# Layer 2's first product as seven half-size products, with prepared factors streamed from DRAM

## The chip, the core and the metric

The kernel runs on one core of a Trainium2 chip. The metric is the device time of one execution in microseconds, as the median of several runs. The core has a matrix engine (TensorE, in the profile PE for matmuls and PEld for weight loads), a vector engine (DVE), a scalar engine (ACT), GpSimd (POOL) and a queue engine (SP), and 16 DMA engines that move data between DRAM and the on-chip memory SBUF. Matmuls write to PSUM, which has eight banks of 512 fp32 numbers per partition. Only DVE and ACT read PSUM here.

## The reference

```python
def _moe_ref(x, w_in, w_out):                 # layer 1
    h = x @ w_in                              # 3072 x 512 @ 512 x 2048
    g = h - np.tanh(h)
    return (g @ w_out).astype(np.float32)     # 3072 x 2048 @ 2048 x 512

def _moe2_ref(x, w_in, w_out, alpha):         # layer 2
    h = x @ w_in
    g = np.maximum(h, 0.0) + alpha * np.minimum(h, 0.0)
    return (g @ w_out).astype(np.float32)

def reference(**kwargs):
    ...
    attn_out = _attn_ref(**attn_kwargs)       # attention in chunks of 32 tokens, 4 x 8 heads x 768 x 64
    x = np.ascontiguousarray(attn_out.transpose(0, 2, 1, 3)).reshape(B * S, H * D)
    x = _moe_ref(x=x, **moe_kwargs)
    return _moe2_ref(x=x, **moe2_kwargs)
```

The weights arrive as 64-bit floats, which the kernel turns into fp32 by integer operations.

## The kernel before

The 3072 tokens are 24 tiles of 128. Both layers work through six blocks of four tiles (512 tokens), and within a block through 16 values of f, each of which stands for 128 of the 2048 hidden units. Layer 1 runs block by block first, then layer 2.

Every fp32 product is made of three matmuls: each operand is split into a high part and a low part (type fp32r), and the passes high x high, high x low and low x high are added up in PSUM (`PASS`). For one block and one f, `emit_h` issues 12 matmuls (four parts of the 512 inputs, three passes), each with 128 weight columns and 512 moving columns, into one bank of `ps_h`. `emit_g` applies the activation: in layer 2 DVE computes prelu in two operations (lines 191 and 194), ACT copies the high part gh (line 197), POOL subtracts it for the low part gl (line 198). `emit_y` issues 12 more matmuls, of 512 columns, into the four banks of `ps_y`, which collect y over the 16 values of f; in layer 2 these are on line 217. In the written order h of the next f comes ahead of y of this one. After the last f of a block `evac_y` copies the four banks out through tiles of the pool t (4 buffers): in layer 1 to y1d in DRAM by ACT's DMA queue, in layer 2 to the output by SP's.

The instructions of each engine are not issued strictly as written: the framework makes a schedule by its own estimates of durations, and an instruction that it holds ready can go ahead of one that it holds late. Each engine then runs its own list in order.

During layer 1 the attention of later tiles runs between the matmuls by a plan of due times (`both`, `emit_soft`, `tok_c`). In the blocks 1 to 4 of layer 1 every second step converts and splits one of the 32 weight tiles of layer 2 (`park`: ACT and three DVE operations in `to_f32`, then ACT and POOL in `split_f32`) and writes it to w2d in DRAM. In block 5 all of them are read back into SBUF (`unpark`), where they stay: 32 tiles of the pool w, which has 34 buffers of 4 KB per partition. For layer 2 `load_x2` reads a block of y1d and `split_x2` splits it into the ring of x operands with four ACT and four DVE operations.

Of the kernel before, what the change touches and what calls it, by code (L numbers as in the profile page):

```python
# [7 lines left out]
FP32 = mybir.dt.float32  # L8
FP32R = mybir.dt.float32r
# [10 lines left out]
PERIOD = 20  # L20
LP, SLACK, LAST_C = 3, 2, 5
SPACE = 6
SCB = 2
FIRST = 1
EARLY_W = (3, 4, 5)
ANCHOR = 'exp'
# [4 lines left out]
XF = 4  # L31
# [5 lines left out]
def chunk_attention_two_ffn_kernel(  # L37
# [27 lines left out]
    def f32(ap):  # L65
        return ap.bitcast(FP32)
# [11 lines left out]
    y1d = dr_p.tile([NTILE, 128, KD, 128], FP32, name="y1d")  # L78
    w2d = [dr_p.tile([128, 2 * 512], FP32, name=f"w2d{i}") for i in range(2 * NF)]

    wts = {}
    raws = {}
# [9 lines left out]
    def to_f32(raw):  # L92
# [12 lines left out]
        s = t_p.tile([128, 512], U32, tag="t", name="s")  # L105
# [9 lines left out]
    def keep(l, f, got):  # L115
        wts[l, f] = (got[0].rearrange("p a (k f) -> p a k f", k=KD), got[1])
# [7 lines left out]
            got.append(w)  # L124
        keep(l, f, got)

    def park(i):
        raw = raws.pop((1, i))
        w = raw.bitcast(FP32R)
        split_f32(to_f32(raw), w[:, 0:512], w[:, 512:1024])  # L130
        nc.sync.dma_start(out=w2d[i], in_=f32(w))

    def unpark(f):
        got = []
        for side in range(2):
            w = w_p.tile([128, 2, 512], FP32R, tag="w", name="wt")
            nc.sync.dma_start(out=f32(w).rearrange("p a n -> p (a n)"), in_=w2d[2 * f + side])
            got.append(w)
        keep(1, f, got)

    ring = [x_p.tile([128, RING, KD, 128], FP32R, name=f"ring{i}") for i in range(2)]

# [80 lines left out]
    def evac_y(l, b, n, t0):  # L223
        ys = yp.pop((l, b))
        for j, y in enumerate(ys):
            if l == 0:
                s = t_p.tile([128, 512], FP32, tag="t", name="ys")[:, :n * 128]
                src, dst = y[:, :n * 128], y1d[t0:t0 + n, :, j, :].rearrange("i p c -> p i c")
                so = s.rearrange("p (i c) -> p i c", i=n)
            else:  # L230
                s = t_p.tile([128, 512], FP32, tag="t", name="ys")
                src, dst, so = y, out[(t0 + j) * 128:(t0 + j + 1) * 128, :], s
            if j % 2 == 0:
                nc.scalar.activation(out=s, in_=src, func=ACTF.Copy)
            else:
                nc.vector.tensor_copy(out=s, in_=src)
            (nc.scalar if l == 0 else nc.sync).dma_start(out=dst, in_=so)

    x2 = {}

    def load_x2(b, n, t0):
        r = stage["x"].tile([128, max(blocks2), KD, 128], FP32, tag="x2", name="x2")
        nc.sync.dma_start(out=r[:, :n], in_=y1d[t0:t0 + n].rearrange("i p k c -> p i k c"))
        x2[b] = r

    def split_x2(b, n):
        r = x2.pop(b)
        for i in range(n):
            o = lambda c: ring[c][:, x0[1][b] + i]
            nc.scalar.activation(out=o(0), in_=r[:, i], func=ACTF.Copy)  # L250
            nc.vector.tensor_tensor(out=o(1), in0=r[:, i], in1=f32(o(0)), op=ALU.subtract)


    astack = ExitStack()
# [41 lines left out]
    def emit_scores(t):  # L296
        s = t % TPS
        kn = kt.pop(t)
        sp = ps_a.tile([128, 512], FP32, tag="a", name="sp")
        for p in range(HP):  # L300
            for c in range(4):
                last["at"] = nc.tensor.matmul(  # L302
                    out=sp[CH * c:CH * c + CH, 128 * p:128 * p + 128],
                    lhsT=qt[t][:, p, CH * c:CH * c + CH],
                    rhs=kn[p // 2][:, :, p % 2, c // 2, CH * (c % 2):CH * (c % 2) + W + NM],
                    start=True, stop=True,
                ).ins
# [5 lines left out]
        sc = aw.tile([128, H, 64], FP32, tag="sc", name="sc", bufs=SCB)  # L313
# [12 lines left out]
    def emit_soft(t):  # L326
        sc = sm.pop(t)
        sg = aw.tile([128, H, 1], FP32, tag="sg", name="sg")
        nc.vector.tensor_reduce(out=sg, in_=sc, op=ALU.add, axis=AX.X)
        nc.vector.tensor_scalar(out=sg, in0=sg, scalar1=1e-9, scalar2=None, op0=ALU.add)  # L330
        nc.vector.reciprocal(out=sg, in_=sg)
        nc.gpsimd.tensor_tensor(
            out=sc, in0=sc, in1=sg.to_broadcast([128, H, 64]), op=ALU.mult
        )
        et = aw.tile([128, H, 2, CH], FP32, tag="et", name="et", bufs=1)
# [70 lines left out]
        last["run"] = last["at"]  # L406

    slots = [(0, b, n, f) for b, n in enumerate(blocks1) for f in range(NF)]
    slots += [(1, b, n, f) for b, n in enumerate(blocks2) for f in range(NF)]
    N1 = len(blocks1)  # L410

    if True:
# [81 lines left out]
        for i, (l, b, n, f) in enumerate(slots):  # L494
            def attn(pos):
                if l == 0:
                    for fn, t in plan.pop(base[b] + pos, []):
                        fn(t)
                    return last.pop("run", None)

            if l == 0 and b == 0:
                more_w()
            if l == 0 and 0 < b < N1 - 1:
                n_park, at_step = divmod((b - 1) * NF + f, 2)
                if at_step == 0:
# [24 lines left out]

# [59 lines left out]
```

## Time and profile before

| | |
|---|---|
| Median of three runs | 1152.1 us (1151.5 to 1152.64) |
| The profiled execution | 1150.37 us |
| Its span, first to last instruction | 1148.5 us |
| PE busy | 1114.7 us (97%) in 6144 matmuls |
| PEld busy | 915.6 us (80%) |
| DVE, ACT, POOL busy | 485.5, 345.5, 363.1 us (42%, 30%, 32%) |
| Moved by DMA | 112.16 MB, 98 GB/s on average |

The profile is of one execution. Its span is a little shorter than the time that counts, since start and end of the program lie around it. Busy time is the union of an engine's records. Matmuls are pipelined, and a matmul's record holds its latency too, so the distance between the starts of matmuls in a row, their pitch, tells what one costs. Idle time on an engine that isn't the bottleneck costs nothing.

### The profile page before, as it was taken

The numbers are of one execution on the slowest core, as the hardware profiler recorded it, in microseconds if no ns is written. First come the engines' busy times: TensorE is split into PE (matmuls) and PEld (weight loads), VectorE is DVE, ScalarE is ACT, GpSimd is POOL, SyncE is SP. The second block draws the span as 40 slices with busy tenths as digits, with TensorE's granted clock in tenths as the row PEclk, the third lists the DMA queues.
The fourth block names the chain that finished last, engine by engine and source line by source line (L and its number), as shares of the span: only waits on it lengthen the run. The fifth ranks groups of instructions, "written<-read, shape, count | busy, mean of one in ns | idle before, by whom it ended". The sixth has DMA issues, their size and how long they took to land.

```text
span 1148.5 us, 15553 instructions
## 1 busy us (share of the span) xinstructions
PE 1114.7 (97%) x6144; PEld 915.6 (80%) x6144; DVE 485.5 (42%) x806; ACT 345.5 (30%) x612; POOL 363.1 (32%) x299
## 2 busy tenths in 40 slices
PE   3798999999999999999999999999999999999998
PEld 3587788888888887887888888888888888888886
DVE  6998635554554544553113224234224224322322
ACT  4665534444343444443222112112112112111111
POOL 4465533433243333332221222222222222222221
PEclk9699999999999999999999999999999999999999
DMA  9772334344444444436665002002002000000000
GB/s 256 260 271 81 104 115 142 125 150 138 147 144 151 140 135 145 149 109 222 204 198 183 1 1 74 1 1 74 1 1 67 7 1 19 19 1 13 25 1 37
DMA packets 53689, 112.16 MB, mean 98 GB/s; under 512 B 7281, under 2 KB 25713, under 8 KB 53617
## 3 DMA queue, kind: packets, MB, share of 16 engines
q1 hardware_dynamic: 40944, 104.89, 28.0%
q10 hardware_dynamic: 12672, 6.29, 1.9%
q8 instruction: 48, 0.79, 0.3%
q14 instruction: 25, 0.20, 0.1%
HBM read 81.80 MB, written 29.36 MB: 97 GB/s over the span
## 4 chain that ended last, share of the span: by engine, by line
PE 88%; DMA 4%; DVE 3%; issue 2%; SPq 1%; POOL 1%; ACT 0%; DVEq 0%; POOLq 0%; ACTq 0%
PE h L173 42%; PE y L217 23%; PE y L212 20%; PE pv L354 2%; PE sp L302 1%; DMA ri<-in_moe_w_in_dram 1%; DMA alpha_sb<-in_moe_alpha_dram 1%; DVE u L102 1%; DMA y1d<-ys 1%; SPq L276 1%; DVE s L106 1%; DVE u L99 1%; DVE ebuf L345 0%; DMA vn<-in_v_dram 0%; DMA w2d<-pk 0%
## 5 line engine op out<-in xcount | busy, mean ns | idle before, releaser
L173 PE MATMUL h<-ring,wt 128*128 128x512 f32 x2304 | 561.2, 392 | 8.9 <-DVE t L189 6.0
L173 PEld LDWEIGHTS h<-ring,wt 128*128 128x128 f32 x2304 | 434.5, 189 | 103.8 <-DVE t L189 8.6
L198 POOL TENSOR_TENSOR gl<-t,gh 128x512 fp32r<-128x512 f32 x192 | 249.2, 1298 | 599.9 <-ACT gh L197 589.3
L197 ACT ACTIVATE gh<-t 128x512 fp32r<-128x512 f32 x192 | 121.2, 631 | 465.7 <-DVE t L194 407.9
L191 DVE TENSOR_SCALAR t<-h,alpha_sb 128x512 f32<-128x512 f32 x96 | 72.1, 751 | 341.6 <-PE h L173 331.8
L212 PE MATMUL y<-gh,wt 128*128 128x512 f32 x768 | 193.7, 391 | 0.0
L217 PE MATMUL y<-wt,gh 128*128 128x512 f32 x768 | 191.6, 389 | 0.0
L212 PEld LDWEIGHTS y<-gh,wt 128*128 128x128 f32 x768 | 143.2, 188 | 31.7 <-issue 2.0
L217 PEld LDWEIGHTS y<-wt,gh 128*128 128x128 f32 x768 | 144.2, 188 | 29.9
L189 DVE TENSOR_TENSOR t<-h,t 128x512 f32<-128x512 f32 x96 | 65.9, 688 | 213.2 <-ACT t L188 198.2
L188 ACT ACTIVATE t<-h 128x512 f32<-128x512 f32 x96 | 57.1, 595 | 184.9 <-PE h L173 169.2
L212 PE MATMUL y<-gl,wt 128*128 128x512 f32 x384 | 105.4, 390 | 0.0
L217 PE MATMUL y<-wt,gl 128*128 128x512 f32 x384 | 104.6, 389 | 0.0
L212 PEld LDWEIGHTS y<-gl,wt 128*128 128x128 f32 x384 | 72.0, 188 | 15.7 <-POOL gl L198 0.4
L217 PEld LDWEIGHTS y<-wt,gl 128*128 128x128 f32 x384 | 72.1, 188 | 15.0
L113 POOL TENSOR_TENSOR pk<-s,pk 128x512 fp32r<-128x512 f32 x32 | 41.6, 1301 | 105.6 <-ACT pk L112 105.6
L194 DVE SCALAR_TENSOR_TENSOR t<-h,t 128x512 f32<-128x512 f32 x96 | 66.4, 691 | 3.2
L113 POOL TENSOR_TENSOR wt<-s,wt 128x512 fp32r<-128x512 f32 x32 | 41.4, 1295 | 39.5 <-ACT wt L112 39.1
L99 DVE TENSOR_SCALAR u<-u 128x512 uint32<-128x512 uint32 x64 | 44.2, 691 | 7.6 <-ACT u L96 7.4
L343 ACT ACTIVATE ebuf<-et 32x256 f32<-32x256 f32 x96 | 39.8, 415 | 8.9 <-DVE et L336 7.4
L345 DVE COPY ebuf<-et 32x256 f32<-32x256 f32 x96 | 39.0, 407 | 1.8
L354 PEld LDWEIGHTS pv<-ebuf,vn 96*64 96x64 f32 x768 | 26.8, 148 | 15.8 <-ACT ebuf L343 7.3
(44 smaller groups left out, 476.8 us busy)
## 6 DMA issues: line engine op xcount, KB each, us to landing
w2d<-pk SPq DMA_DIRECT2D x32, 512.0 KB, 2.6
wt<-w2d SPq DMA_DIRECT2D x32, 512.0 KB, 3.8
vn<-in_v_dram SPq DMA_DIRECT2D x24, 384.0 KB, 4.2
ri<-in_moe_w_in_dram SPq DMA_DIRECT2D x16, 512.0 KB, 6.8
ro<-in_moe_w_out_dram SPq DMA_DIRECT2D x16, 512.0 KB, 7.7
pk<-in_moe_w_in_dram SPq DMA_DIRECT2D x16, 512.0 KB, 3.6
pk<-in_moe_w_out_dram SPq DMA_DIRECT2D x16, 512.0 KB, 3.5
kbuf<-in_k_dram SPq DMA_DIRECT2D x80, 96.0 KB, 3.4
```

The lines of the kernel that those rows point to most:

```text
L99: nc.vector.tensor_scalar(out=u, in0=u, scalar1=3, scalar2=None, op0=ALU.logical_shift_left)
L113: nc.gpsimd.tensor_tensor(out=lo, in0=v, in1=f32(hi), op=ALU.subtract)
L173: last["ffn"] = nc.tensor.matmul(out=h, lhsT=wi[:, a, kk, :], rhs=ring[c][:, s0:s0 + n, kk, :], start=(i == 0), stop=(i == 3 * KD - 1),).ins
L188: nc.scalar.activation(out=t, in_=h, func=ACTF.Tanh)
L189: nc.vector.tensor_tensor(out=t, in0=h, in1=t, op=ALU.subtract)
L191: nc.vector.tensor_scalar(out=t, in0=h, scalar1=0.0, scalar2=alpha_sb[:, f:f + 1], op0=ALU.min, op1=ALU.mult)
L194: nc.vector.scalar_tensor_tensor(out=t, in0=h, scalar=0.0, in1=t, op0=ALU.max, op1=ALU.add)
L197: nc.scalar.activation(out=gh, in_=t, func=ACTF.Copy)
L198: nc.gpsimd.tensor_tensor(out=gl, in0=t, in1=f32(gh), op=ALU.subtract)
L212: mm = nc.tensor.matmul(out=yp[l, b][j][:, :n * 128], lhsT=wo[:, a, j * 128:(j + 1) * 128], rhs=g[c], start=first, stop=final,)
L217: mm = nc.tensor.matmul(out=yp[l, b][j], lhsT=g[a][:, j * 128:(j + 1) * 128], rhs=wo[:, c, :], start=first, stop=final,)
L354: last["at"] = nc.tensor.matmul(out=pv[D * j:D * j + D, 128 * p + 64 * a:128 * p + 64 * a + 64], lhsT=vt[t][:, a, D * h:D * h + D], rhs=eb ...
```

## The change

Layer 1 stays as it is but for where some attention tiles lie. In layer 2, h is computed for two values of f at once (a pair) by a scheme with seven products instead of eight. The pair's weights are cut into quadrants (two values of f by two halves of the 512 inputs), the block of x into quadrants (two halves of the inputs by two halves of the 512 tokens). A product of two quadrants is six matmuls with 128 weight columns and 256 moving columns: two parts of the 256 inputs, three passes. Four of the weight factors and four of the x factors are sums or differences of quadrants.

- In blocks 1 to 4 of layer 1 `park_in` and `park_sum` make the seven weight factors of each pair and write them, split, to w2i; `park_out` does for w_out what `park` did, to w2o.
- In layer 2 the w_out tiles are resident, eight in pool w and eight in the memory of the ring. The seven factors of a pair are read from w2i for each block anew, in four transfers, three pairs ahead (`load_in`).
- x of a block is read as two tiles, four DVE subtractions make its sums (`sums_x2`), and ACT and POOL split the seven factors (`split_x2`).
- `pair_h` issues the products in the order 1, 6, 2, 5, 7, 3, 4. They share two PSUM banks (`ps_h2`): 1 and then 2 on top of it in the first, 6 in the second, 5 and then 3 in the first, 7 and then 4 in the second. DVE and ACT add what has to be added on the way out. `pair_y` issues the 24 matmuls of y in six groups of four, which are written between the products of the next pair.
- `evac_y` issues all its transfers from ACT's queue. y1d is laid out by blocks. The attention's et lies in pool t, sc in pool w for the first tiles and later in a single buffer.

```diff
-    w2d = [dr_p.tile([128, 2 * 512], FP32, name=f"w2d{i}") for i in range(2 * NF)]
+    y1d = dr_p.tile([len(blocks1), 128, KD, 512], FP32, name="y1d")
+    w2i = [dr_p.tile([128, 7 * 512], FP32, name=f"w2i{i}") for i in range(NF // 2)]
+    w2o = [dr_p.tile([128, 2 * 512], FP32, name=f"w2o{i}") for i in range(NF)]
...
+    def park_sum(p, half):
+        lo, hi = slice(0, 256), slice(256, 512)
+        v0, v1 = sw[0], sw[1]
+        s = t_p.tile([128, 512], FP32, tag="t", name="sm")
+        if half == 0:
+            nc.vector.tensor_tensor(out=s[:, hi], in0=v1[:, lo], in1=v1[:, hi], op=ALU.add)
+            nc.vector.tensor_tensor(out=s[:, lo], in0=s[:, hi], in1=v0[:, lo], op=ALU.subtract)
+            sw["s2"] = s
...
+        w = w_p.tile([128, 1024], FP32R, tag="w", name="ws")
+        split_f32(s, w[:, 0:512], w[:, 512:1024])
+        c = 1024 * (1 + half)
+        nc.sync.dma_start(out=w2i[p][:, c:c + 1024], in_=f32(w))
...
     def evac_y(l, b, n, t0):
...
-            (nc.scalar if l == 0 else nc.sync).dma_start(out=dst, in_=so)
+            nc.scalar.dma_start(out=dst, in_=s)
...
+    WSLOT = {1: 0, 2: 1, 6: 2, 5: 3, 7: 4, 3: 5, 4: 6}
+    ORDER = (1, 6, 2, 5, 7, 3, 4)
...
+    def load_in(i, q):
+        p = i % (NF // 2)
+        n = 2 if q < 3 else 1
+        w = w_p.tile([128, 2, n, 256], FP32R, tag="w", name="wi2")
+        nc.sync.dma_start(
+            out=f32(w).rearrange("p a s n -> p (a s n)"),
+            in_=w2i[p][:, 1024 * q:1024 * q + 512 * n])
+        win[i, q] = w
...
+    def split_x2(b, m):
+        src = {1: 11, 2: 21, 3: 22}.get(m)
+        src = xin[b, m] if src is None else part(b, src)
+        o = w_p.tile([128, 2, 2, 256], FP32R, tag="w", name="xop")
+        nc.scalar.activation(out=o[:, 0], in_=src, func=ACTF.Copy)
+        nc.gpsimd.tensor_tensor(out=o[:, 1], in0=src, in1=f32(o[:, 0]), op=ALU.subtract)
+        xop[b, m] = o
...
+    def product(h, i, m, first, last_one):
+        b = i // (NF // 2)
+        s = WSLOT[m]
+        w, x = win[i, s // 2][:, :, s % 2], xop[b, m]
+        j = 0
+        for kt in range(2):
+            for a, c in PASS:
+                nc.tensor.matmul(
+                    out=h, lhsT=w[:, a, 128 * kt:128 * kt + 128], rhs=x[:, c, kt, :],
+                    start=(first and j == 0), stop=(j == 5), skip_group_check=True,
+                )
+                j += 1
+
+    def prelu(t, h, f):
+        nc.vector.tensor_scalar(
+            out=t, in0=h, scalar1=0.0, scalar2=alpha_sb[:, f:f + 1], op0=ALU.min, op1=ALU.mult
+        )
+        nc.vector.scalar_tensor_tensor(
+            out=t, in0=h, scalar=0.0, in1=t, op0=ALU.max, op1=ALU.add
+        )
...
+        def bank(m):
+            d[m] = ps_h2.tile([128, 512], FP32, tag="h2", name="h2")[:, 0:256]
+            return d[m]
...
+        def s1():
+            product(bank(1), i, 1, True, False)
+            d["s"] = tmp("hs")
+            nc.scalar.activation(out=d["s"], in_=d[1], func=ACTF.Copy)
+
+        def s6():
+            product(bank(6), i, 6, True, True)
+            d["u"] = tmp("hu")
+            add(d["u"], d[6], d["s"])
+
+        def s2():
+            product(d[1], i, 2, False, True)
+            d["t0"] = t_p.tile([128, 512], FP32, tag="t", name="t0")
+            prelu(d["t0"][:, 0:256], d[1], f)
+
+        def s5():
+            product(bank(5), i, 5, True, False)
+            d["v"] = tmp("hv")
+            add(d["v"], d[5], d["u"])
+
+        def s7():
+            product(bank(7), i, 7, True, False)
+            d["c"] = tmp("hc", 512)
+            add(d["c"][:, 256:512], d[7], d["v"])
+
+        def s3():
+            product(d[5], i, 3, False, True)
+            c = tmp("hd")
+            add(c, d[5], d["u"])
+            prelu(d["t0"][:, 256:512], c, f)
+            gs[1, i, 0] = split_g(d["t0"])
+
+        def s4():
+            product(d[7], i, 4, False, True)
+            add(d["c"][:, 0:256], d[7], d["u"])
+            t = t_p.tile([128, 512], FP32, tag="t", name="t1")
+            prelu(t, d["c"], f + 1)
+            gs[1, i, 1] = split_g(t)
...
+            if i + 3 < N2:
+                for q in range(4):
+                    load_in(i + 3, q)
+            hs = pair_h(i + 1) if i + 1 < N2 else []
+            ys = pair_y(i)
+            for k in range(7):
+                if hs:
+                    hs[k]()
+                if k < 6:
+                    ys[k]()
+                if k in (1, 4) and p >= 1 and work:
+                    work.pop(0)()
...
+            if p == P2 - 1:
+                evac_y(1, b, 4, start2[b])
```

## Rows read from the trace of the kernel before

**Rows 1.** The page: engines, granted clock in 40 slices, chain by engine.
```profile
PE 1114.7 (97%) x6144; PEld 915.6 (80%) x6144; DVE 485.5 (42%) x806; ACT 345.5 (30%) x612; POOL 363.1 (32%) x299
...
PEclk9699999999999999999999999999999999999999
...
PE 88%; DMA 4%; DVE 3%; issue 2%; SPq 1%; POOL 1%; ACT 0%; DVEq 0%; POOLq 0%; ACTq 0%
```
**Rows 2.** Windows by stage: length, engines' busy time (instructions), clock, DMA share, GB/s.
```profile
130.00:530.00 400.00, 399.32 (x2646) 326.74 (x2645) 200.33 (x361) 170.74 (x310) 143.91 (x116) 1.00 0.44 138
530.00:620.00 90.00, 89.49 (x396) 73.78 (x395) 16.66 (x26) 24.63 (x42) 22.90 (x18) 1.00 0.64 210
640.00:1140.00 500.00, 500.00 (x2208) 414.15 (x2207) 152.63 (x210) 71.75 (x118) 118.39 (x91) 1.00 0.05 17
```
**Rows 3.** Waits of PE after 500 us: total us, times, longest us.
```profile
PE h L173 <- DVE t L189: 0.5, 1, 0.5
```
**Rows 4.** Timeline of PE in layer 2: start, length, line, count.
```profile
739.44 2.88 PE L173 MATMUL h<-ring,wt 128*128 128x512 f32 x12
...
744.88 2.88 PE L173 MATMUL h<-ring,wt 128*128 128x512 f32 x12
```
**Rows 5.** The window from 41.2 to 45.4 us, columns as in rows 2.
```profile
41.20:45.40 4.20, 4.20 (x11) 3.30 (x10) 4.13 (x8) 3.53 (x8) 1.35 (x2) 0.50 0.97 332
```
**Rows 6.** Timeline of PE in that window; one record there lasts 0.63 us.
```profile
41.63 4.47 PE L173 MATMUL h<-ring,wt 128*128 128x512 f32 x10
```
**Rows 7.** Timeline from 49.9 to 50.8 us: DVE, weight loads, PE.
```profile
49.91 0.68 DVE L189 TENSOR_TENSOR t<-h,t 128x512 f32<-128x512 f32 x1
...
50.65 0.30 PEld L173 LDWEIGHTS h<-ring,wt 128*128 128x128 f32 x2 [2.36 <-DVE t L189]
...
50.65 0.50 PE L173 MATMUL h<-ring,wt 128*128 128x512 f32 x1 [1.94 <-DVE t L189]
```
**Rows 8.** Timeline of weight loads, pv of one tile.
```profile
268.76 1.01 PEld L354 LDWEIGHTS pv<-ebuf,vn 96*64 96x64 f32 x32 [0.35 <-issue]
```
**Rows 9.** The page's groups: busy us, mean ns; idle before.
```profile
L173 PE MATMUL h<-ring,wt 128*128 128x512 f32 x2304 | 561.2, 392 | 8.9 <-DVE t L189 6.0
L173 PEld LDWEIGHTS h<-ring,wt 128*128 128x128 f32 x2304 | 434.5, 189 | 103.8 <-DVE t L189 8.6
L198 POOL TENSOR_TENSOR gl<-t,gh 128x512 fp32r<-128x512 f32 x192 | 249.2, 1298 | 599.9 <-ACT gh L197 589.3
```
**Rows 10.** Timeline of the last h and its prelu, from 1136 us.
```profile
1136.56 1.52 PE L173 MATMUL h<-ring,wt 128*128 128x512 f32 x6
...
1138.20 0.75 DVE L191 TENSOR_SCALAR t<-h,alpha_sb 128x512 f32<-128x512 f32 x1 [3.96 <-PE h L173]
1138.98 0.69 DVE L194 SCALAR_TENSOR_TENSOR t<-h,t 128x512 f32<-128x512 f32 x1
...
1139.79 0.63 ACT L197 ACTIVATE gh<-t 128x512 fp32r<-128x512 f32 x1 [4.81 <-DVE t L194]
```
**Rows 11.** Groups by form from 60 to 530 us: copies of 256 elements.
```profile
L345 DVE COPY ebuf<-et 32x256 f32<-32x256 f32 x76 | 32.2, 423 | 1.4
```
**Rows 12.** Timeline around the end of layer 2's first block.
```profile
704.86 2.98 DVE L251 TENSOR_TENSOR ring<-x,ring 128x512 fp32r<-128x512 f32 x3
...
705.75 1.54 POOL L198 TENSOR_TENSOR gl<-t,gh 128x512 fp32r<-128x512 f32 x1 [4.61 <-ACT gh L197]
...
706.80 3.34 PE L173 MATMUL h<-ring,wt 128*128 128x512 f32 x14
...
712.70 3.79 PE L173 MATMUL h<-ring,wt 128*128 128x512 f32 x16
...
715.35 0.75 DVE L191 TENSOR_SCALAR t<-h,alpha_sb 128x512 f32<-128x512 f32 x1 [1.55 <-DMA out_dram<-ys]
716.32 0.62 PE L217 MATMUL y<-wt,gh 128*128 128x512 f32 x2
```
**Rows 13.** Line 251 from 640 to 1140 us: duration in ns, min/median/max.
```profile
L251 DVE TENSOR_TENSOR ring<-x,ring x16: 682/686/1779, 703.7 to 967.2; 128x512 fp32r<-128x512 f32 x16
```
**Rows 14.** DMA issues from 640 to 1140 us: KB each, us to landing.
```profile
out_dram<-ys SPq DMA_DIRECT2D x20, 256.0 KB, 2.5
```

More of the change, by code (lines that the diff above doesn't have):

```diff
@@ L125, in split_w, with park_in @@
         keep(l, f, got)
-    def park(i):
-        raw = raws.pop((1, i))
+    sw = {}
+    def park_in(f):
+        raw = raws.pop((1, 2 * f))
+        v = aw.tile([128, 512], FP32, tag="v", name="wv")
+        v = to_f32(raw, v)
+        w = raw.bitcast(FP32R)
+        p, odd = divmod(f, 2)
+        sw[odd] = v
+        if odd:
+            split_f32(v[:, 256:512], w[:, 0:256], w[:, 256:512])
+            nc.sync.dma_start(out=w2i[p][:, 3072:3584], in_=f32(w)[:, 0:512])
+        else:
+            split_f32(v, w[:, 0:512], w[:, 512:1024])
+            nc.sync.dma_start(out=w2i[p][:, 0:1024], in_=f32(w))
@@ L129, in park, with park_out @@
+    def park_out(f):
+        raw = raws.pop((1, 2 * f + 1))
         w = raw.bitcast(FP32R)
         split_f32(to_f32(raw), w[:, 0:512], w[:, 512:1024])
[L131 to L139, printed above, removed]
+        nc.sync.dma_start(out=w2o[f], in_=f32(w))
@@ new lines, in park_step @@
+    def park_step(n):
+        p, k = divmod(n, 8)
+        f = 2 * p
+        if k == 0:
+            if p == 0:
+                load_raw(1, 0, "pk")
+                return
+            park_in(f)
+            load_raw(1, 2 * f + 2, "pk")
+        elif k == 1:
+            if p == 0:
+                park_in(f)
+                load_raw(1, 2 * f + 2, "pk")
+            else:
+                park_in(f + 1)
+        elif k == 2:
+            if p == 0:
+                park_in(f + 1)
+            else:
+                park_sum(p, 0)
+        elif k == 3:
+            if p == 0:
+                park_sum(p, 0)
+            else:
+                park_sum(p, 1)
+        elif k == 4:
+            if p == 0:
+                park_sum(p, 1)
+            load_raw(1, 2 * f + 1, "pk")
+        elif k == 5:
+            park_out(f)
+            load_raw(1, 2 * f + 3, "pk")
+        elif k == 6:
+            park_out(f + 1)
+        elif p + 1 < NF // 2:
+            load_raw(1, 2 * f + 4, "pk")
@@ L237, in evac_y @@
-            (nc.scalar if l == 0 else nc.sync).dma_start(out=dst, in_=so)
[L239 to L251, printed above, removed]
+            s = t_p.tile([128, 512], FP32, tag="t", name="ys")
@@ new lines, in evac_y, with load_out @@
+            dst = y1d[b, :, j, :] if l == 0 else out[(t0 + j) * 128:(t0 + j + 1) * 128, :]
+            if j % 2 == 0:
+                nc.scalar.activation(out=s, in_=y, func=ACTF.Copy)
+            else:
+                nc.vector.tensor_copy(out=s, in_=y)
+            nc.scalar.dma_start(out=dst, in_=s)
+    WSLOT = {1: 0, 2: 1, 6: 2, 5: 3, 7: 4, 3: 5, 4: 6}
+    ORDER = (1, 6, 2, 5, 7, 3, 4)
+    wo2 = {}
+    win = {}
+    xop = {}
+    xin = {}
+    def load_out(f):
+        if f < NF // 2:
+            w = w_p.tile([128, 2, 512], FP32R, tag="w", name="wo2")
+        else:
+            g = f - NF // 2
+            s0 = [x0[0][b] for b in range(len(blocks1) - 1, len(blocks1))][0]
+            free = 4 - s0
+            r, c = divmod(g % 4, 2)
+            s = (free if g < 4 else s0) + 2 * c
+            w = ring[r][:, s:s + 2].rearrange("p (a i) k c -> p a (i k c)", a=2)
+        nc.sync.dma_start(
+            out=f32(w), in_=w2o[f].rearrange("p (a n) -> p a n", a=2))
+        wo2[f] = w
@@ new lines, in load_in, with load_x2 @@
+    def load_in(i, q):
+        p = i % (NF // 2)
+        n = 2 if q < 3 else 1
+        w = w_p.tile([128, 2, n, 256], FP32R, tag="w", name="wi2")
+        nc.sync.dma_start(
+            out=f32(w).rearrange("p a s n -> p (a s n)"),
+            in_=w2i[p][:, 1024 * q:1024 * q + 512 * n])
+        win[i, q] = w
+    def load_x2(b):
+        for j in range(2):
+            r = stage["x"].tile([128, 2, 512], FP32, tag="x2", name="x2", bufs=2)
+            nc.sync.dma_start(out=r, in_=y1d[b, :, 2 * j:2 * j + 2, :])
+            xin[b, j] = r
@@ new lines, in part, with sums_x2 @@
+    def part(b, which):
+        return xin[b, which // 10 - 1][:, :, 256 * (which % 10 - 1):256 * (which % 10)]
+    def sums_x2(b, half):
+        t = stage["x"].tile([128, 2, 2, 256], FP32, tag="xt", name="xt", bufs=2)
+        sub = lambda o, p, q: nc.vector.tensor_tensor(out=o, in0=p, in1=q, op=ALU.subtract)
+        if half == 0:
+            sub(t[:, 0], part(b, 12), part(b, 11))
+            sub(t[:, 1], part(b, 22), t[:, 0])
+            xin[b, 5], xin[b, 6] = t[:, 0], t[:, 1]
+        else:
+            sub(t[:, 0], part(b, 22), part(b, 12))
+            sub(t[:, 1], part(b, 21), xin[b, 6])
+            xin[b, 7], xin[b, 4] = t[:, 0], t[:, 1]
@@ new lines, in pair_y, with four @@
+    def pair_y(i):
+        b, p = divmod(i, NF // 2)
+        if p == 0:
+            yp[1, b] = [ps_y.tile([128, 512], FP32, tag="y", name="y") for _ in range(4)]
+        todo = []
+        for odd in range(2):
+            f = 2 * p + odd
+            for n, (a, c) in enumerate(PASS):
+                def four(f=f, odd=odd, n=n, a=a, c=c):
+                    for j in range(4):
+                        nc.tensor.matmul(
+                            out=yp[1, b][j], lhsT=gs[1, i, odd][a][:, j * 128:(j + 1) * 128],
+                            rhs=wo2[f][:, c, :], start=(f == 0 and n == 0),
+                            stop=(f == NF - 1 and n == 2),
+                        )
+                todo.append(four)
+        order = [todo[0], todo[1], todo[2], todo[3], todo[4], todo[5]]
+        return order
```

97 lines of the change are left out of this document (63 added, 34 removed).

## Prediction

> **What bounds the kernel now.** I read the page first: TensorE is busy 97% of the span, every other engine 42% or less, at a granted clock of 0.9 or more of the 2.4 GHz level in all slices but one, and the chain that ended last lies on PE for 88% [rows 1]. Next the windows by stage: from 130 us on PE stands still for little more than 1 us, and between 640 and 1140 us, in layer 2, DVE is busy 153 of 500 us, ACT 72, POOL 118 and DMA 5% [rows 2]. PE's list of waits after 500 us has one entry, 0.5 us [rows 3]. So layer 2 costs what its matmuls cost in a row. The timeline of PE gives their pitch: h begins at 739.44, the next h at 744.88, 24 matmuls between, 226.7 ns each [rows 4].
>
> What makes up 226.7? At the 2.4 GHz level 512 columns are 213.3 ns; 13.3 are left. At the 1.2 GHz level (granted clock 0.50 [rows 5]) ten matmuls of line 173 take 4.47 us together, the last of them 0.63 in its record, so they start (4.47 - 0.63) / 9 = 427 ns apart [rows 6], which is 512 columns at 1.2 GHz and nothing more. So the 13.3 ns are an addition that shows only at the fast level. The load of the next weights is recorded with 188 ns, but that is mostly latency: after a pause two loads lie within 0.30 us, so the second began some 0.30 - 0.19 = 0.11 us after the first, 108 ns in the records [rows 7], and 32 loads of 138 ns for pv fit into 1.01 us [rows 8]. The loads hide behind 226.7 ns now.
>
> **The change part by part.** *h in layer 2.* 1152 of the 2304 matmuls of line 173 [rows 9] go: 1152 x 0.2267 = 261.1 us. In come 48 pairs x 7 products x 6 = 2016 matmuls with 256 columns and the same 128-column weights. Seven eighths of the columns, but 7/4 as many matmuls and loads: all hangs on their pitch. No row has 256 columns. From below, a matmul can't follow faster than the weight loads, 108 ns [rows 7]; if all of today's pitch were proportional, 113.3. From above, nothing hides and the load's recorded 188 ns set the pitch. The addition being absent at half clock, I read it as a fixed piece per instruction: 106.7 + 13.3 = 120 ns, nearest to the rows with the same weights and type [rows 4, 6]. That is 2016 x 0.120 = 241.9 us: **-19.2 us**. Seven products beat eight only below 261.1 / 2016 = 129.5 ns.
>
> The Trainium skill (TensorE: Matmul & The Clock Gate, Back-to-back issue gap) gives N / 2.4 + 2.5 ns for a matmul without its weight load, 109.2 ns at 256 columns. By that the term would be 41.0 us instead of 19.2. The trace disagrees at 512 columns: the rule gives 215.8, the row 226.7.
>
> *Waits inside a pair.* Written order: product 1, four y matmuls, 6, four, 2, four, 5, four, 7, four, 3, four, 4. Product: 6 x 0.12 = 0.72 us, four y: 0.91, a pair 10.48. The seven share two PSUM banks, and DVE must read between. Prices: from the last column to DVE's start 0.28 us (six matmuls from 1136.56 end at 1137.92, DVE starts at 1138.20); between two DVE operations 0.03; DVE to ACT 0.12 [rows 10]; DVE to PE 0.06 (49.91 + 0.68 to 50.65) [rows 7]. A DVE operation on 256 elements lies between half of 0.69 and the 0.42 that the 256-element copies take; I take 0.42 to 0.43, and 0.49 for the one that took 0.75 on 512 [rows 10, 11].
> - Product 5 goes into product 1's bank, which prelu must have read after product 2: 0.28 + 0.49 + 0.03 + 0.43 + 0.06 = 1.29 us, 1.40 if the weight load waits too. Four y cover 0.91. Open: 0.38 to 0.49, 18 to 23.5 us over 48 pairs, if PE keeps the written order. But the twelve y matmuls of the odd half are ready and may go ahead. In the trace PE doesn't keep the written order when something is late: h runs in groups of 14 and 16 instead of 12, y's first eight with gh begin as a group of 2 [rows 12], and PE waits for none of it [rows 3]. I take +1 us; bounds 0 and 23.5.
> - y's first four need gh from product 3: 0.28 + 0.43 + 0.03 + 0.49 + 0.03 + 0.43 + 0.12 + 0.63 + 0.06 = 2.50 us (2.61 with the load), covered by four y and two products, 2.35. Product 6 may fill, but its bank comes free only 0.28 + 0.43 + 0.06 = 0.77 us after product 4, when y is just due. I take 0.08 a pair, +4 us; bounds 0 and 12.
> - gl on POOL (1.3 [rows 9]) has over 2 us in hand, also the odd half's. Engine loads per pair: DVE 9 x 0.43 + 1.44 = 5.3 of 10.5 us, ACT 1.7, POOL 2.6, and per block 4 DVE subtractions, 7 ACT copies and 7 POOL subtractions for x: none near full.
>
> DVE operations with two SBUF operands meet POOL: L251's usually take 686 ns, at most 1779, and the stretched ones lay beside a POOL operation of 1.54 us instead of 1.3 [rows 9, 12, 13]. Product 4's and 3's prelu now read SBUF twice. Product 4's has 2 us in hand; product 3's meets POOL only when x is split, in 4 of 8 pairs, for which the 0 to 12 us above have room.
>
> The Trainium skill (SBUF — State Buffer, SBUF: two separate sides) says that such a DVE operation and one of GpSimd exclude each other for a whole instruction. The maximum of L251 agrees. Charged in full in each of the 20 pairs with a split, at 1.1 us, it would cost 22 us.
>
> *Block ends.* Five times y's banks must be copied out between two blocks while the short pool t also holds prelu results; a copy can wait for an out transfer (2.5 us to landing) [rows 14], as DVE does now for 1.55 us [rows 12]. Products 6 and 2 fill 1.44 us. Bounds 0 and 2.5 each, taken 0.6: +3 us. Out transfers move from SP's queue to ACT's: each issue stands in front of gh there; the last four cost some +0.5 at the end. SP, rid of them, queues only loads behind waits for free w buffers.
>
> *Between the layers.* The first pair has only the last y of layer 1 between its products: +1.5 us, bounds 0 and 4.
>
> *Weights streamed.* 7 x 512 x 4 bytes x 128 partitions = 1.84 MB a pair, 175 GB/s at 10.5 us, with x and out some 200. The queue moved 210 GB/s at a share of 0.64 between 530 and 620 us [rows 2] and 332 at 0.97 [rows 5]. A set is asked for two pairs, 21 us, ahead and takes 5.5 us at that rate: hidden.
>
> *Layer 1.* 8 x 4 x 0.42 = 13.5 us more DVE, 8 ACT, 16 POOL, one more transfer a pair, single sc, et in pool t. All of it lies between 130 and 530 us, where DVE is busy 200 of 400 us, ACT 171, POOL 144 and PE full [rows 2]: 0, at most 5.
>
> Sum: -19.2 + 1 + 4 + 3 + 0.5 + 1.5 = **-9.2 us**. The profiled execution took 1150.37 us (span 1148.5), so 1141.2; the median of the runs, 1152.1, lies 1.7 above it: **1143 us**.
>
> **The rivals.**
> - *The addition shrinks with the columns.* 113.3 ns gives 2016 x 0.0067 = 13.5 us more gain, 1130 us; at the floor of 108 ns 24 more, 1119. For it: 13.3 is a sixteenth of 213.3. Against: 427 ns at half clock, exactly the columns. 0.24. The skill's 109.2 ns lies in this case, at 1121 us.
> - *Slower: PE keeps the written order* and stands before product 5 and before y. At 20 and 9 us for the two waits instead of 1 and 4 this gives 1168; half of it 1155. It decides from 0.19 us a pair on. For it: two banks only, and a schedule made without the chip need not know DVE's 1.29 us; in the trace PE once waited 1.94 us for DVE [rows 7]. Against: [rows 12]. 0.18.
> - *Weight loads set the pitch.* Load and matmul are both about 107 ns long, so any slip adds. 130 ns: 1163; 188: 1280. For it: loads busy 80% already [rows 1]. Against: the overlapping loads [rows 7, 8]. 0.08.
> - *Weights arrive late*, since a set's loads wait on SP for buffers of a set in use. One us a pair is 48 us, 1191. For: every w buffer is taken late in a block. Against: 21 us ahead. 0.05.
>
> **How the numbers follow.** The forecast's own case has 0.45, with a range of its own of 1133 to 1150. The range from 1120 to 1164 takes in the shrinking addition almost to its floor and the written order up to most of its price; out of it lie part of that order, the 188 ns and late weights, with 0.02 below and 0.17 above. Faster by over 0.2% (what a measurement here can tell from no change) means under 1149.8: 0.40 of the forecast's case, 0.24, and 0.02 of the written order, 0.66. Within 0.2%: 0.09, from the edges of the forecast's case and of the written order. Slower: 0.25.
>
> **What would show it.** Right: 256-column matmuls 120 ns apart in a product; a pair near 10.6 us against 10.88 now; y groups of more than four before product 5; PE without waits in layer 2; DMA share near 0.65 there. Wrong: a pitch of 113 or below, or above 130; PE waits released by DVE some 48 times before product 5 or y's gh; waits for transfers of w2i; PE no longer full before 530 us.

## The result: slower by 0.6%, and the profile after

| | before | after |
|---|---|---|
| Median of the runs (lowest to highest) | 1152.11 us (1151.5 to 1152.64) | 1158.97 us (1157.43 to 1161.16) |
| The profiled execution, its span | 1150.37, 1148.5 us | 1161.16, 1159.4 us |
| Last y of layer 1 to last y of layer 2 | 517.25 us | 524.01 us |

The ratio of after to before is 1.0061, with an interval of 1.0042 to 1.008: slower, where 1143 us and a faster kernel were forecast; outside the forecast's own case and inside its range. From the last y of layer 1 to the last y of layer 2 the change takes 6.8 us more.

The page of after: engines, granted clock, chain by engine.
```profile
PE 1111.7 (96%) x7008; PEld 944.7 (81%) x7008; DVE 621.4 (54%) x1174; ACT 380.5 (33%) x694; POOL 438.5 (38%) x357
...
PEclk9899999999999999999999999999999999999999
...
PE 82%; DVE 7%; DMA 4%; issue 4%; ACT 1%; SPq 0%; POOL 0%; DVEq 0%; ACTq 0%; POOLq 0%
```
DVE has come into the chain, from 3% to 7%, though it is busy only 54% of the span. The windows of after, with the columns of [rows 2]:
```profile
130.00:530.00 400.00, 398.11 (x2627) 323.56 (x2627) 222.87 (x396) 178.00 (x326) 164.41 (x134) 1.00 0.47 150
640.00:1140.00 500.00, 491.46 (x3015) 438.26 (x3014) 263.71 (x533) 99.04 (x182) 165.35 (x126) 1.00 0.52 176
```
Layer 1 still fills PE with all the extra factor work in it. In layer 2 PE, which never stood still before, has holes of 8.5 us in 500. PE's waits after 620 us, where [rows 3] had one of 0.5 us:
```profile
PE h L371 <- DVE hu L395: 6.3, 10, 0.6
PE y L456 <- ACT gh L388: 2.7, 8, 1.6
```
Ten waits for the tile hu, two in each of the first five blocks. A stretch of PE's timeline without one:
```profile
762.79 3.82 PE L371 MATMUL h<-xop,wi 128*128 128x256 f32 x30
766.45 2.00 PE L456 MATMUL y<-ring,gh 128*128 128x512 f32 x8
768.29 0.88 PE L371 MATMUL h<-xop,wi 128*128 128x256 f32 x6
769.00 1.09 PE L456 MATMUL y<-ring,gl 128*128 128x512 f32 x4
769.93 1.75 PE L456 MATMUL y<-ring,gh 128*128 128x512 f32 x7
771.52 0.88 PE L371 MATMUL h<-xop,wi 128*128 128x256 f32 x6
772.24 0.40 PE L456 MATMUL y<-ring,gh 128*128 128x512 f32 x1
```
Six h matmuls take 772.24 - 771.52 = 0.72 us: 120 ns, as forecast; over whole products the median is 119.6 a matmul. A pair takes 10.61 us, forecast 10.6. But two pairs in each of the blocks 0 to 4 take 12.02 to 12.05. One of these, by engine (start, length):
```profile
775.02 1.30 POOL L357 TENSOR_TENSOR xop<-x,xop 128x512 fp32r<-128x512 f32 x1 [6.29 <-ACT xop L356]
776.28 1.47 POOL L357 TENSOR_TENSOR xop<-xt,xop 128x512 fp32r<-128x512 f32 x1
777.70 1.48 POOL L389 TENSOR_TENSOR gl<-t,gh 128x512 fp32r<-128x512 f32 x1
...
775.38 1.22 DVE L381 SCALAR_TENSOR_TENSOR t<-hd,t 128x256 f32<-128x256 f32 x1
776.52 1.50 DVE L378 TENSOR_SCALAR t<-hc,alpha_sb 128x512 f32<-128x512 f32 x1
778.06 1.67 DVE L381 SCALAR_TENSOR_TENSOR t<-hc,t 128x512 f32<-128x512 f32 x1
779.65 0.41 DVE L395 TENSOR_TENSOR hu<-h,hs 128x256 f32<-128x256 f32 x1
...
773.75 3.48 PE L371 MATMUL h<-xop,wi 128*128 128x256 f32 x27
777.38 2.11 PE L456 MATMUL y<-ring,gh 128*128 128x512 f32 x8
780.12 1.71 PE L371 MATMUL h<-xop,wi 128*128 128x256 f32 x11 [0.63 <-DVE hu L395]
```
Read it from the end. PE waits for the add that empties product 6's bank (line 395, 779.65 + 0.41 = 780.06). That add needs nothing that is late but its turn: on DVE it stands behind three prelu operations of 1.22, 1.50 and 1.67 us. Product 6 had ended at about 776.3 (773.75 + 21 x 0.12), so with the prediction's 0.28 us the add was ready at about 776.5, and it came 3.1 us later. Each of the three ends 0.27 to 0.55 us after a POOL operation does (776.32, 777.75, 779.18). How long they usually are, by form (min/median/max in ns):
```profile
L378 DVE TENSOR_SCALAR t<-hc,alpha_sb x46: 478/480/1510, 644.4 to 1137.1; 128x512 f32<-128x512 f32 x46
L381 DVE SCALAR_TENSOR_TENSOR t<-hd,t x46: 414/416/1228, 641.1 to 1136.7; 128x256 f32<-128x256 f32 x46
L381 DVE SCALAR_TENSOR_TENSOR t<-hc,t x46: 680/693/1668, 644.9 to 1137.6; 128x512 f32<-128x512 f32 x46
```
The ten long pairs are exactly those in which all three are stretched; in the other pairs none of the three is.

The sum for layer 2, from the distances between the starts of all matmuls: h 2016 x 119.6 - 261.1 = -20.0 us; a slower pitch after each change of the column count +3.3; waits +21.1; and less of layer 2's h was done before layer 1's last y (24 matmuls of 120 ns against 22 of 227), +2.1. That gives +6.5 where 6.8 was measured. The 2.1 us are work that lies on the other side of the mark, not time lost; without them layer 2 loses 4.4 us by this sum. Of the waits, a long pair has 1.43 us: 0.79 at product 5, 0.42 at two y matmuls whose gh is late, 0.24 at the first matmuls behind product 5's wait; ten pairs, 14.3 us. (The list of waits shows only 9.0 of the 21.1 us: a matmul's record, 0.28 us at 256 columns, is longer than its pitch of 0.12 and covers part of a gap.) The other 6.8 are mostly 0.42 at each of five block ends, 1.8 before the last y, and 65 ns at product 1's second matmul in 41 pairs.

### The profile page after: what moved, and what is told of

Same layout as the page of the kernel before. It is cut to its first block, busy times and chain, and to the rows that moved or that the text cites. A ratio compares the mean times of both kernels' runs of the same rounds, so it can differ in the third digit from the quotient of the medians.

```text
span 1159.4 us, 18520 instructions
## 1 busy us (share of the span) xinstructions
PE 1111.7 (96%) x7008; PEld 944.7 (81%) x7008; DVE 621.4 (54%) x1174; ACT 380.5 (33%) x694; POOL 438.5 (38%) x357
## 4 chain that ended last, share of the span: by engine, by line
PE 82%; DVE 7%; DMA 4%; issue 4%; ACT 1%; SPq 0%; POOL 0%; DVEq 0%; ACTq 0%; POOLq 0%
PE y L456 21%; PE y L277 20%; PE h L238 20%; PE h L371 18%; DVE t L378 2%; PE pv L570 2%; PE sp L514 1%; DVE t L381 1%; DMA ri<-in_moe_w_in_dram 1%; DMA alpha_sb<-in_moe_alpha_dram 1%; DVE u L102 1%; DVE u L99 1%; DVE s L106 1%; DMA qn<-in_q_dram 0%; DMA vn<-in_v_dram 0%
## 5 line engine op out<-in xcount | busy, mean ns | idle before, releaser
L238 PE MATMUL h<-ring,wt 128*128 128x512 f32 x1152 | 284.3, 395 | 4.5 <-DVE t L254 2.4
L371 PEld LDWEIGHTS h<-xop,wi 128*128 128x128 f32 x2016 | 263.3, 190 | 22.5 <-DVE hu L395 10.5
L371 PE MATMUL h<-xop,wi 128*128 128x256 f32 x2016 | 270.3, 285 | 6.3 <-DVE hu L395 6.3
L238 PEld LDWEIGHTS h<-ring,wt 128*128 128x128 f32 x1152 | 217.2, 190 | 53.5 <-DVE t L254 4.1
L389 POOL TENSOR_TENSOR gl<-t,gh 128x512 fp32r<-128x512 f32 x96 | 127.4, 1341 | 295.5 <-ACT gh L388 280.8
L456 PE MATMUL y<-wo,gh 128*128 128x512 f32 x384 | 100.9, 394 | 1.5 <-ACT gh L388 0.8
L456 PE MATMUL y<-ring,gh 128*128 128x512 f32 x384 | 99.2, 393 | 2.4 <-ACT gh L388 1.9
L456 PEld LDWEIGHTS y<-ring,gh 128*128 128x128 f32 x384 | 70.5, 188 | 16.8 <-ACT gh L388 3.6
L456 PEld LDWEIGHTS y<-wo,gh 128*128 128x128 f32 x384 | 70.1, 188 | 16.9 <-ACT gh L388 3.5
L395 DVE TENSOR_TENSOR hd<-h,hu 128x256 f32<-128x256 f32 x48 | 20.4, 425 | 79.0 <-PE h L371 78.9
L395 DVE TENSOR_TENSOR hc<-h,hv 128x256 f32<-128x256 f32 x48 | 20.3, 424 | 76.0 <-PE h L371 76.0
```

The costliest lines, as they stand in the source:

```text
L238: last["ffn"] = nc.tensor.matmul(out=h, lhsT=wi[:, a, kk, :], rhs=ring[c][:, s0:s0 + n, kk, :], start=(i == 0), stop=(i == 3 * KD - 1),).ins
L371: nc.tensor.matmul(out=h, lhsT=w[:, a, 128 * kt:128 * kt + 128], rhs=x[:, c, kt, :], start=(first and j == 0), stop=(j == 5), skip_group_c ...
L389: nc.gpsimd.tensor_tensor(out=gl, in0=t, in1=f32(gh), op=ALU.subtract)
L395: add = lambda o, p, q: nc.vector.tensor_tensor(out=o, in0=p, in1=q, op=ALU.add)
L456: nc.tensor.matmul(out=yp[1, b][j], lhsT=gs[1, i, odd][a][:, j * 128:(j + 1) * 128], rhs=wo2[f][:, c, :], start=(f == 0 and n == 0), stop= ...
```

## The experiments

Theory A: GpSimd's split of x shuts VectorE's prelu out of SBUF, the add behind it is late, and PE, with two banks for seven products, waits for that add. Rivals: two banks or DVE's total work are too much whatever GpSimd does; the smaller matmul or PE's order costs it; the attention's moved buffers do. The first four kernels ran on one chip with before at 1152.21 us.

**The change again**, as it is.

> The changed kernel once more, for a second profile. Its first profile shows a pair of layer 2 at 10.6 us where nothing disturbs it, but two pairs in each of the first five blocks at 12.0, and the start of layer 1 4.7 us later than before. If the two long pairs belong to the program, they come again at the same places: 48 pairs, ten of them 1.4 us longer. If the late start belongs to the program, the first h of layer 1 again begins near 43.6 us and not near 38.9; if it is the execution's, it moves by some us. Time 1157 to 1161.

1159.4 us, 1.0063 (1.0048 to 1.0078). Layer 2 took 524.1 us, with the same ten long pairs. Layer 1's first h came at 42.7 us and its last y at 626.8, in the first profile at 43.6 and 629.9, in before at 38.9 and 625.9.

**x's low parts on DVE**
```diff
-        nc.gpsimd.tensor_tensor(out=o[:, 1], in0=src, in1=f32(o[:, 0]), op=ALU.subtract)
+        nc.vector.tensor_tensor(out=o[:, 1], in0=src, in1=f32(o[:, 0]), op=ALU.subtract)
```


> The low parts of x's seven factors are made on DVE instead of POOL, nothing else. Theory A, POOL's subtractions for x and gl shut out DVE's prelu on operands that both lie in SBUF: the long pairs (ten times 1.43 us) shrink by more than half, time 1145 to 1152. Rival B, DVE is simply late there because two PSUM banks leave it no time: it gets 7 x 0.69 us more work in each block, so the long pairs stay or grow, 1158 to 1164.

1147.82 us, 0.9964 (0.9951 to 0.9977). DVE got more work and PE less to wait for: the long pairs fell to 10.8 to 11.3 us, layer 2 to 513.9. The waits for hu are gone; what is left of PE's list after 620 us:
```profile
PE y L456 <- ACT gh L388: 1.6, 1, 1.6
PE h L371 <- DVE t L381: 0.2, 1, 0.2
```

**No x work**: blocks 1 to 5 use block 0's x factors, so that loading, adding and splitting of x are left out there.
```diff
-        w, x = win[i, s // 2][:, :, s % 2], xop[b, m]
+        w, x = win[i, s // 2][:, :, s % 2], xop[0, m]
...
-                work = x2_work(b + 1) if b + 1 < len(blocks2) else []
+                work = []
```


> Blocks 1 to 5 of layer 2 use block 0's x factors: loading, summing and splitting x for them is left out. If the work for x makes the long pairs, by whatever way, all pairs take 10.6 us but for the block ends, 14 to 16 us less: 1142 to 1145. If they come from the streamed weights or from the two banks, they stay: 1155 to 1160.

1144.89 us, 0.9941 (0.9924 to 0.9957). Every pair inside a block takes 10.6 us, layer 2 509.9: all of the x work together costs 14.2 us, what the ten long pairs lose.

**Four product banks**: products 5 and 7 take the two banks that layer 1 used.
```diff
-            d[m] = ps_h2.tile([128, 512], FP32, tag="h2", name="h2")[:, 0:256]
+            pool, tag = (ps_h2, "h2") if m in (1, 6) else (ps_h, "h")
+            d[m] = pool.tile([128, 512], FP32, tag=tag, name="h2")[:, 0:256]
```


> Products 5 and 7 (and 3 and 4 on top of them) go into the two banks that layer 1 used for h and that layer 2 leaves idle, so that no product waits for a bank that prelu still reads. Theory A: DVE's operations are stretched as before, and PE waits for what they deliver: 1154 to 1160. Rival B, the wait for a bank is what costs: PE's waits for DVE go, 1143 to 1150.

1141.03 us, 0.9903 (0.9886 to 0.992). Theory A as I had put it missed: I expected the stretched prelu to cost about as much. It is there, and longer on average (703 and 903 ns in after):
```profile
L378 DVE TENSOR_SCALAR t<-hc,alpha_sb 128x512 f32<-128x512 f32 x47 | 49.5, 1053 | 4.1 <-DVE hc L395 0.5 <-DMA y1d<-ys 0.4
L381 DVE SCALAR_TENSOR_TENSOR t<-hc,t 128x512 f32<-128x512 f32 x47 | 45.3, 964 | 0.0
```
But the time is below rival B's 1143 to 1150, and PE's list after 620 us holds one entry:
```profile
PE y L457 <- ACT gh L388: 0.5, 1, 0.5
```
Layer 2 takes 503.3 us, eight pairs 84.4, 10.55 each, x split and block ends included. So the lock-out alone is not the loss; it becomes one where the next product waits for the bank behind it.

**Four banks, and x's low parts on DVE** (both edits above; before in this and the next three: 1153.08 us).

> Both edits together: x's low parts on DVE and four banks for the products. Four banks alone left PE without waits in layer 2, at 10.55 us a pair. If the banks alone already hide DVE's stretched operations, the other edit adds nothing: 1139 to 1142. If DVE and POOL shutting each other out still costs something of its own, it comes out 2 to 5 us lower, 1135 to 1138.

1139.96 us, 0.9892 (0.9876 to 0.9908), the fastest, 1% below before. One edit gave 18 us, the other 12, and both some 20 (7 over before against 13 under it); the interval overlaps that of four banks alone. So both cut at the same loss. Four banks also take away the small waits and those at block ends, which x's low parts on DVE leave: layer 2 takes 503.3 us with the first and 513.9 with the second.

**Fixed order, y in runs of twelve**, on top of that kernel: four products, 12 y, three products, 12 y, each matmul issued after the one ahead of it.
```diff
-                if k < 6:
-                    ys[k]()
+                if k in (3, 6):
+                    for go in (ys[:3] if k == 3 else ys[3:]):
+                        go()
```


> As the run with both edits, but PE's order in layer 2 is fixed: four products, twelve y, three products, twelve y. What is tested is the pitch of y's matmuls: in the changed kernel the first seven after a switch from 256 to 512 columns are up to 8 ns slower, some 27 ns a switch, and from the eighth on they take 226.7 again. With two switches a pair instead of three or four, a pair should take 42 x 0.1196 + 24 x 0.2267 + 2 x 0.027 = 10.52 us against 10.55, and with no gaps at block ends the time is 1137 to 1141. If the slow pitch comes from something else that runs beside y (DVE, DMA), the excess per y stays as it is.

1163.96 us, 1.0097 (1.0082 to 1.0112): missed. Fewer changes of column count do save, as PE's timeline shows:
```profile
763.49 2.00 PE L466 MATMUL y<-wo,gh 128*128 128x512 f32 x8
765.33 1.07 PE L466 MATMUL y<-wo,gl 128*128 128x512 f32 x4
766.24 3.11 PE L380 MATMUL h<-xop,wi 128*128 128x256 f32 x24
```
12 y in 766.24 - 763.49 = 2.75 us, 0.03 us over 12 x 226.7, at one change instead of several. But a usual pair takes 10.65 us, not the 10.52 expected: small waits at products 2 and 4 outweigh the saving. And PE can no longer put something else ahead of a late product. Layer 2 takes 528.4 us, 24.6 more than in the kernel with both edits; PE's list after 620 us shows about half of that as waits for the copy of product 1:
```profile
PE h L380 <- ACT hs L418: 12.5, 15, 1.0
```

**The written order**, on top of the change: the rival of the prediction, with PE made to keep it.
```diff
+            with tc.issue_after(last["layer2"]):
+                last["layer2"] = go().ins
```


> The changed kernel with PE held to the written order in layer 2 (product 1, four y, 6, four y, 2 and so on). By the prediction's chain, product 5 then stands 0.38 to 0.49 us in every pair and y's first four 0.15 to 0.26 us; together 25 to 35 us over 48 pairs, of which the changed kernel shows almost none outside the long pairs: 1175 to 1192. Rival: the written order is as good as the schedule's (1155 to 1162), and the chain's durations are overestimated.

1198.81 us, 1.0403 (1.0385 to 1.042). Slower by more than expected, and not where expected. Inside a pair:
```profile
799.70 0.88 PE L380 MATMUL h<-xop,wi 128*128 128x256 f32 x6
800.41 1.09 PE L465 MATMUL y<-ring,gh 128*128 128x512 f32 x4
801.34 0.87 PE L380 MATMUL h<-xop,wi 128*128 128x256 f32 x6
802.05 1.08 PE L465 MATMUL y<-ring,gl 128*128 128x512 f32 x4
```
No wait; such a pair takes 10.55 us. The loss lies in pairs with x work (11.6 and 12.7 us) and at block ends (17.3 to 18.7 us), where nothing may go ahead of y while its banks are copied out. PE's waits after 620 us:
```profile
PE y L465 <- DVE ys L296: 17.6, 11, 2.7
PE y L465 <- ACT gh L397: 8.9, 12, 1.0
PE y L465 <- ACT ys L294: 5.8, 11, 1.8
```
There the clock falls too: PE's timeline behind one block end, and two windows, columns as in [rows 2].
```profile
731.06 1.48 PE L380 MATMUL h<-xop,wi 128*128 128x256 f32 x6
732.34 1.91 PE L465 MATMUL y<-wo,gh 128*128 128x512 f32 x4
```
```profile
725.00:730.00 5.00, 1.50 (x3) 0.56 (x3) 2.78 (x4) 1.56 (x4) 2.29 (x2) 0.90 0.88 281
730.00:735.00 5.00, 4.53 (x16) 4.05 (x17) 0.84 (x2) 0.00 (x0) 0.00 (x0) 0.50 0.21 79
```
At a granted clock of 0.50, the 1.2 GHz level, six h take 732.34 - 731.06 = 1.28 us, 213 ns each. PE had been busy 1.5 of the five microseconds ahead.

**Before, with layer 2's h matmuls cut into two of 256 columns**: the pitch alone.
```diff
-        for kk in range(KD):
+        parts = ((0, n),) if l == 0 else ((0, n // 2), (n // 2, n))
+        for lo, hi in parts:
+            for kk in range(KD):
```


> The kernel before, with each matmul of h in layer 2 cut into two of 256 columns (eight half-size products, no sums, no streamed weights): 2304 matmuls instead of 1152. This prices the short matmul by itself. At 119.6 ns each: 275.6 - 261.1 = +14.5 us, and y after each switch 27 ns slower per twelve, 96 x 0.027 = +2.6 us: 1168 to 1170. At 113.3 ns, the proportional reading, +0 and +2.6: 1154 to 1156.

1169.97 us, 1.0152 (1.0136 to 1.0167): hit. PE has no wait after 620 us, and
```profile
761.60 3.04 PE L175 MATMUL h<-ring,wt 128*128 128x256 f32 x24
764.48 2.00 PE L221 MATMUL y<-wt,gh 128*128 128x512 f32 x8
```
24 h take 2.88 us, 120 ns each. The fixed piece per matmul is there without the scheme too.

**Before, with the attention's buffers of the change** (this and the next ran on one chip, before at 1152.01 us).
```diff
-        sc = aw.tile([128, H, 64], FP32, tag="sc", name="sc", bufs=SCB)
+        if t <= NS:
+            sc = w_p.tile([128, H, 64], FP32, tag="w", name="sc")
+        else:
+            sc = aw.tile([128, H, 64], FP32, tag="sc", name="sc", bufs=1)
...
-        et = aw.tile([128, H, 2, CH], FP32, tag="et", name="et", bufs=1)
+        et = t_p.tile([128, 512], FP32, tag="t", name="et")
+        et = et.rearrange("q (h s n) -> q h s n", h=H, s=2)
```


> The kernel before, with one thing of the change alone: the attention's score and exponent tiles come from the buffers that the change gives them. No product, factor or load is changed. Theory A (the loss of the change lies in layer 2, in VectorE's stretched prelu; the 3 us by which the first matmul of layer 1 starts later come from the attention's buffers): the first matmul of h in layer 1 starts at 41.5 to 43.5 us in place of 38.9, and most of that is made up by the end of layer 1; time 1151 to 1155 us, no more than 3 us over the kernel before. Rival (the buffers cost what the change lost): 1157 to 1161 us, with the layer's end as much later. If the first matmul starts at 38.9 us as before, the later start belongs to the other edits.

1151.52 us, 1.0 (0.999 to 1.0009). Layer 1's first h came at 41.1 us, a little before the 41.5 to 43.5 expected (38.9 in before), its last y at 623.8. This profile is of the fastest of ten executions, 1148.26 us. By the times the buffers cost nothing that can be told.

**Prelu's sums in PSUM**: the change with its two product banks and GpSimd's splits, hc and hd in the two banks that layer 1 used.
```diff
-            d["c"] = tmp("hc", 512)
+            d["c"] = ps_h.tile([128, 512], FP32, tag="h", name="hc")
...
-            c = tmp("hd")
+            c = ps_h.tile([128, 512], FP32, tag="h", name="hd")[:, 0:256]
```


> The changed kernel with its two product banks, x's low parts on GpSimd as it has them, and one thing else: the two running sums of a group that prelu reads (c for h and d for h) are kept in PSUM and not in SBUF, so that prelu reads and writes less of SBUF. Theory A (GpSimd's splits shut VectorE out of SBUF while VectorE reads both operands there, and the add queued behind the stretched prelu holds product 5 back): the ten pairs of 12.0 us in blocks 0 to 4 fall to 10.6 to 10.9 us, prelu beside a split takes 0.5 to 0.7 us in place of 1.5, time 1143 to 1148 us. Rival (two banks are too few for the products, or VectorE has too much to do, whatever GpSimd does beside it): the long pairs stay, 1155 us or more.

1153.75 us, 1.0014 (1.0002 to 1.0026): the time missed, between the two theories. The stretching is gone, as the forms in the trace show (min/median/max):
```profile
L378 DVE TENSOR_SCALAR t<-hc,alpha_sb x47: 739/743/751, 640.1 to 1137.2; 128x512 f32<-128x512 f32 x47
L381 DVE SCALAR_TENSOR_TENSOR t<-hc,t x47: 679/681/692, 640.9 to 1138.0; 128x512 f32<-128x512 f32 x47
L381 DVE SCALAR_TENSOR_TENSOR t<-hd,t x46: 411/414/425, 650.7 to 1136.9; 128x256 f32<-128x256 f32 x46
```
With GpSimd working as before (L389 1291 ns on the mean, 1341 in after, L357 in the same pairs), not one prelu operation is stretched: maxima of 1510, 1668 and 1228 ns became 751, 692 and 425. No pair of 12 us is left. But layer 2 takes 518.1 us, since most pairs now hold small waits at products 1, 6 and 4 (0.07 to 0.14 us in 46 pairs, 0.7 at product 4 once a block): prelu's first operation on hc takes 0.74 us from PSUM and 0.48 from SBUF, which would account for part of them, but no run shows that apart. So the rival holds in part: with two banks smaller delays on DVE, without GpSimd, reach PE too. The time of its profiled execution, 1150.77 us, is the lowest of ten.

**What moved along with the edits.** Each edit makes the framework's schedule anew. In after the add for hu stands behind prelu's last operation on hc in every pair. It stands ahead of it in the ten formerly long pairs with x's low parts on DVE, in 36 pairs, these ten among them, with the sums in PSUM, and in 46 with four banks, as here:
```profile
771.86 0.42 DVE L395 TENSOR_TENSOR hu<-h,hs 128x256 f32<-128x256 f32 x1
772.19 1.54 DVE L381 SCALAR_TENSOR_TENSOR t<-hc,t 128x512 f32<-128x512 f32 x1
```
So some of the gain of these three kernels can come from the add's earlier place in DVE's list, up to 1.67 us of its 3.1 us of waiting in a long pair; how much, no run shows. The kernel without x work keeps after's order in every pair: there no prelu operation is stretched and no pair is long. What starts the loss is thus shown; how it divides between the stretching, the add's place and the shared bank is not.

## Why the prediction was wrong

**Right.** The pitch: 119.6 ns for 120, so the term is -20.0 us for -19.2; neither the shrinking addition (113.3) nor weight loads setting the pitch (130 and more) came about, and the price of the split pitch alone was hit. Streamed weights are hidden: PE has no wait for w2i, whose loads land in 4.2 us at the median; the DMA share is 0.52, forecast 0.65. y does run in groups of eight before product 5. The block ends: the two pairs around one take 12.45 + 9.10 us, 0.33 over two usual ones, five times that is 1.7 us (taken 3).

**The step that failed** is the sentence that "Product 4's has 2 us in hand", and with it the x split at nothing in "the 0 to 12 us above". Product 4's prelu itself has that time: in the long pairs no y waited for its gh or gl. What stands behind prelu on DVE has not. The add that frees product 6's bank waited its turn behind three operations of 4.4 us together, usually 1.6, and product 5 waited for the bank. The waits that this made, for which the sum had +1 before product 5 and room in +4 before y, measured 14.3 us: about 10 at product 5 and 4 at y. That the +4 before y came out so near is luck: it was 0.08 us in every pair, and came as 0.42 in ten, for gh of product 3, whose prelu was stretched too. I had asked who waits for the late operation, and not who waits for the next one on its engine.

**A wrong picture beside it.** Prediction and description have product 5 in product 1's bank. Product 5 gets product 6's bank, which is free after one add; product 7 then has product 1's. The kernel with the written order shows it, where product 5 begins while prelu still reads product 1's bank, up to 813.82 us:
```profile
813.40 0.42 DVE L390 SCALAR_TENSOR_TENSOR t<-h,t 128x256 f32<-128x256 f32 x1
813.54 0.88 PE L380 MATMUL h<-xop,wi 128*128 128x256 f32 x6
```
Product 5 stands there without a wait, so the 0.38 to 0.49 us a pair of "PE keeps the written order" don't exist. That rival foretold a slower kernel for a wrong reason: the changed kernel does not keep the written order, and held to it takes 1198.81 us, not the 1168 (by its own sum 1167) of the rival.

**The rule that I weighed and didn't choose.** The prediction had the Trainium skill (SBUF — State Buffer, SBUF: two separate sides) at 22 us, for 20 pairs of 1.1. The trace agrees with the rule: after 640 us each of the 30 stretched prelu operations ends 0.28 or 0.55 us after one of GpSimd's, and those that read PSUM are never stretched (L378 on h: 467 to 486 ns). The charge of 22 us took twice as many pairs as were hit and less for each: 10 of 1.43. With four banks operations are still stretched and PE doesn't wait, so the price depends on what waits behind. For that the Trainium skill has a sentence too (Perfetto Trace Analysis, Matmuls): independent groups should rotate through different banks, so that emptying one overlaps the next. The runs agree: four banks for two, with the schedule that goes with them, are worth 18 us here.

**Not foreseen**: 3.3 us for the changes of column count, and most of 6.8 us of waits outside the long pairs. The +1.5 for the first pair's waits did not come: PE's list has none between 530 and 640 us. The +0.5 at the end was for issues on ACT's queue; what came instead is 1.8 us before the last pair's y, which waits for gh with no product left to fill in. Layer 1, taken at 0 with 5 at most, ended 0.9 and 4.0 us later in two profiles, with 2.1 us less of layer 2's work in it; the buffers alone did not do it. What else moves it between executions stays open; the granted clock of the page's second slice differs too, 0.8 in after and 0.6 in before.

## What to carry to other kernels

When an operation on an engine may be stretched, follow its queue: the next instruction there pays, and then whoever waits for that one. Products that are read between accumulations may need more banks than the dependencies ask for: with two, prelu operations that took 2.8 us longer on DVE became 1.43 us of PE's waits in a pair; with four PE did not wait for them. And look where the schedule puts the operation that frees a bank: it can move when something else is edited. Splitting a matmul pays by measured pitch, not by columns: here 256 columns cost 53% of 512.

## What the runs showed of the hardware

- A fixed piece of some 13 ns per matmul at the 2.4 GHz level: 226.7 ns for 512 columns, 119.6 for 256. At the 1.2 GHz level there is none: 427 ns for 512 [rows 6], 213 for 256 in the kernel with the written order.
- After a change from 256 to 512 columns the first y matmuls start 233, 235, 229, 232 and 230 ns apart, then some 227: about 27 ns a change, with no wait in the profile. In the kernel before, where h has 512 columns too, y behind h starts every 227 ns from its first matmul on; cutting h into 256 columns there brings the slower starts.
- Shut out beside GpSimd is also an operation with a single tensor operand, if that lies in SBUF: L378 on hc took 478 ns at least and 1510 at most; with the operand in PSUM 739 to 751, slower than undisturbed from SBUF but never stretched. The two-operand L381 on hc takes about 680 ns at least either way, and is stretched (to 1668) only with both operands in SBUF.
- A stretched operation ends a fixed time after GpSimd's: 0.28 us for those on hd and for L378 on hc, 0.55 us for L381 on hc, within some 5 ns in the 30 cases after 640 us.
